# The last group's components of an inverse transform: by direct SBUF rows instead of through DRAM

## The chip, the cores and the metric

The kernel runs on one NeuronCore of a Trainium2 chip. The metric is device time in microseconds of one execution; the kernel before and the changed kernel are compared by the medians of their runs. TensorE (PE) does the matmuls, VectorE (DVE) and ScalarE (ACT) move results out of PSUM and do the elementwise work, GpSimd (POOL) helps and issues DMAs, and SyncE (SP) issues DMAs only. SP, ACT and POOL each have a DMA queue of their own.

## The reference

Two spectral layers and two MLP layers alternate on a 2048 x 1024 bfloat16 activation:

```python
def _A_ref(x, w_r, w_i):                    # spectral filter
    X = rfft2(x.astype(float32), axes=(-2, -1))
    X = X * (w_r + 1j * w_i)
    return irfft2(X, s=(S, D), axes=(-2, -1)).astype(bfloat16)

def _B_ref(x, w1, b1, w2):                  # MLP with Mish
    h = einsum("bsd,df->bsf", x, w1) + b1
    sp = log1p(exp(-abs(h))) + where(h > 0, h, 0)
    return einsum("bsf,fd->bsd", h * tanh(sp), w2)

x = A_x                                     # (1, 2048, 1024)
x = x + _A_ref(layernorm(x), A_w_r, A_w_i)
x = x + _B_ref(layernorm(x), B_w1, B_b1, B_w2)
x = x + _A_ref(layernorm(x), A_w_r, A_w_i)
x = x + _B_ref(layernorm(x), B_w1, B_b1, B_w2)
```

## The kernel before

**The spectral layer.** The two-dimensional transform is done as matmuls against tables of cosines and sines. 2048 = 16 x 128 and 1024 = 8 x 128 are split into a short and a long factor, so the forward transform and the inverse have three steps each. `s1` is the short step over both axes; its result has 128 components, 16 for each of 8 groups g. For each group, `s2` and `s3` do the long steps, the filter is multiplied in, and `i1` and `i2` undo the long steps. `i4` undoes the short step for all groups together.

**Stages of one group.** `s3` (L737) multiplies, ACT copies the result out of PSUM (L750), and four DVE operations (L754 to L761) apply the filter. `i1(g, i)` (L764; matmuls at L772) runs twice, for i = 0 and 1; each time ACT copies 1024 columns, two PSUM banks, into the buffer V (L779). `i2(g, half)` (L781; matmuls at L793 and L811) runs twice too. Half 0 makes components 0 to 7 of the group, half 1 components 8 to 15, two banks each time. ACT copies them into U (L821); for three groups, of which the last is one, DVE copies the second half (L819).

**The turn.** U has positions l on its 128 partitions and holds 16 components r of 128 values n. `i4` needs the components on the partitions: UT has partition 8r + g, and l and n along its row. So U is stored to the DRAM tensor `u_d` and read back in another order. For groups 0 to 6, `u_turn` stores all of U on SP's queue and then reads back the group before (`u_back(g - 1)`), so one group's read-back runs beside the next group's work. Group 7 has nothing to hide behind. Each of its halves is stored by ACT as soon as it is copied (`u_turn`, L830), and `u_last` (L842) reads them back by position quarters: two DMAs of two quarters each for half 0, and four DMAs of one quarter for half 1, on SP and ACT.

`i4` (L945; matmuls at L951) takes 32 positions at a time at first, with `r_ut[q]` as the resource of the q-th quarter of positions, so its first call waits for the first quarter alone.

**Order.** The order of the stages is written out by hand in `order_A`; each string is stage, group, half (5 is `i2`), and it ends "... 460 461 370 371 560 561 470 471 570 571". Every engine takes its instructions in program order[...]. `op`, `group` and `dma` compute the waits: a read waits for all writes of a resource, a write for its readers and writers, and `parts` for what was there before `begin()`.

**Around the end of the layer.** After 571, `spin(26, 0)` issues 26 matmuls of 512 columns into PSUM bank 0 whose result nobody reads (L629), so that PE doesn't idle:

```python
self.spin(26, 0)
if li == 0:
    self.op(self.pool, lambda e: e.tensor_copy(self.B1[:], self.B1h[:]), ...)
...
while self.w1_next < 28 * li + 6:
    self.load_w1(after=self.r_ut)
```

The copy of the MLP's bias B1 on POOL follows in the first layer only. The six loads of W1 on SP wait for all of UT. Then `layer_B` starts with `i4`; DVE adds its result to the residual XS (L973), takes the statistics of the layer norm, and the MLP's matmuls `mm1` (L1041) and `mm2` (L1058) follow.

**PSUM.** `pair()` deals the eight banks out as four pairs in turn; each stage's result takes a pair, and a stage waits until its pair has been read.

**A row from SBUF to SBUF** is used in one other place of the kernel: `xr_direct` (L532) moves sixteen pieces of 16 KB from 64 partitions into one partition each, over the queues of SP, ACT and POOL, at the start of the second spectral layer.

Of the kernel before, what the change touches and what calls it, by code (L numbers as in the profile page):

```python
# [7 lines left out]
P = 128  # L8
# [171 lines left out]
class KB:  # L180
# [122 lines left out]
    def build(self):  # L303
# [9 lines left out]
        with ExitStack() as es:  # L313
# [25 lines left out]
            self.r_ident, self.r_m, self.r_mt, self.r_fd, self.r_bd = (Res(n) for n in ("id", "m", "mt", "fd", "bd"))  # L339
            self.r_b1, self.r_eps, self.r_warm = Res("b1"), Res("eps"), Res("warm")  # L340
            self.r_ud = [Res(f"ud{i}") for i in range(8)]
            self.r_ud7 = [Res(f"udh{i}") for i in range(2)]
            self.r_wd = [Res(f"wd{i}") for i in range(8)]
            self.r_xnd = [Res(f"xnd{i}") for i in range(16)]
            self.npair = 0
# [322 lines left out]
    def layer_A(self, li):  # L668
# [95 lines left out]
        def i1(g, i):  # L764

            ps, banks, _ = self.pair()
            yk, bt, v = YK[(2 * g + i) % 6], BT[g % 3], V[g % 2]
            t = bt.ap[:, i, :]
            fns = []
            for c in range(4):  # L770
                for part in range(2):
                    fns.append(lambda e, c=c, part=part: e.matmul(  # L772
                        ps[:, c * 256:(c + 1) * 256], yk.ap[:, part, c * P:(c + 1) * P], t[:, (128, 0)[part]:(384, 256)[part]],
                        start=(part == 0), stop=(part == 1)))
            self.group(fns, reads=[yk.res, bt.res], writes=banks)
            if i == 0:
                v.res.begin()
            src = ps.rearrange("p (c n) -> p c n", n=P)
            self.op(act, lambda e: e.activation(v.ap[:, :, i, :], src, ACT.Copy), reads=banks, parts=[v.res])  # L779

        def i2(g, half):  # L781

            ps, banks, _ = self.pair()
# [4 lines left out]
            def cls(kd, re, im):  # L788
                t = kd * 3 * P
                for dst, stats in ((re, (0, 2)), (im, (1, 0))):  # L790
                    for part in range(2):
                        c = t + stats[part] * P
                        fns.append(lambda e, dst=dst, part=part, c=c: e.matmul(  # L793
                            dst, BD[:, c:c + P], mov(kd, part), start=(part == 0), stop=(part == 1)))
            if half == 0:
                cls(0, ps[:, 0:256], ps[:, 256:512])
                cls(1, ps[:, 512:768], ps[:, 768:1024])
            else:
                cls(2, ps[:, 0:256], ps[:, 512:768])

                t = 9 * P
                if g == 0:
                    outs = [[(i, part, (0, 2)[part]) for part in range(2)] for i in range(2)]
                else:
                    outs = [[(0, 0, 0), (0, 1, 2), (1, 0, 0), (1, 1, 2)], [(0, 0, 1), (0, 1, 0), (1, 0, 2), (1, 1, 3)]]
                for m, terms in enumerate(outs):
                    for n, (i, part, tab) in enumerate(terms):
                        for kd in range(2):
                            rows = slice(64 * kd, 64 * kd + 64)
                            dst = ps[:, 512 * kd + 256 + m * P:512 * kd + 256 + (m + 1) * P]  # L810
                            fns.append(lambda e, dst=dst, rows=rows, i=i, part=part, tab=tab, n=n, last=len(terms) - 1: e.matmul(  # L811
                                dst, BD[rows, t + tab * P:t + (tab + 1) * P], v.ap[rows, 6 + part, i, :],
                                start=(n == 0), stop=(n == last)))
            self.group(fns, reads=[v.res, self.r_bd], writes=banks)
            if half == 0:
                u.res.begin()
            dst = u.ap[:, 8 * half:8 * half + 8, :].rearrange("p a b -> p (a b)")
            if (g, half) in ((3, 1), (5, 1), (7, 1)):
                self.op(dve, lambda e: e.tensor_copy(dst, ps), reads=banks, parts=[u.res])  # L819
            else:  # L820
                self.op(act, lambda e: e.activation(dst, ps, ACT.Copy), reads=banks, parts=[u.res])  # L821
# [1 line left out]
        def u_turn(g, half):  # L823

            u = U[g % 3]
            if g == 7:
                h = slice(8 * half, 8 * half + 8)
                if half == 0:
                    u_back(6)
                self.dma(act, self.u_d[g][:, h, :], u.ap[:, h, :], f"uwh{half}", reads=[u.res], writes=[self.r_ud7[half]])  # L830
                if half:
                    u_last()
            elif half:
                self.dma(sp, self.u_d[g], u.ap, f"uw{g % 3}", reads=[u.res], writes=[self.r_ud[g]])
                if g:
                    u_back(g - 1)
# [2 lines left out]
            self.dma(sp, self.UT.ap[g:P:8, :, :], self.u_d[g].rearrange("l r n -> r l n"), f"usp{g % 3}",  # L839
                     reads=[self.r_ud[g]], parts=self.r_ut)  # L840

        def u_last():  # L842

            def back(prog, half, q, n):
                l = slice(32 * q, 32 * q + 32 * n)
                self.dma(prog, self.UT.ap[7 + 64 * half:P if half else 64:8, l, :], self.u_d[7][l, 8 * half:8 * half + 8, :].rearrange("l r n -> r l n"),
                         f"ul{half}{q}", reads=[self.r_ud7[half]], parts=self.r_ut[q:q + n])
            back(sp, 0, 0, 2)
            back(sp, 0, 2, 2)
            for q in range(4):  # L850
                back((act, sp)[q % 2], 1, q, 1)

        self.s1(li)
        Z = ring("Z", 6, 2 * K, [2, 512])
# [10 lines left out]
        for stage, g, h in self.order_A():  # L865
# [15 lines left out]
            elif stage == 4:  # L881
                i1(g, h)
                if h and g < 6:
                    load_btabs(g + 2)
            else:
                i2(g, h)
                u_turn(g, h)
        self.spin(26, 0)
        if li == 0:
            self.op(self.pool, lambda e: e.tensor_copy(self.B1[:], self.B1h[:]), reads=[self.r_b1h], writes=[self.r_b1])  # L890
        self.w1_buf = [self.alloc(f"W1_{i}", (self.W1_OFF + i * 4096, 140 * K + (i - 4) * 4096)[i > 3], [8, 256]) for i in range(6)]
# [372 lines left out]
```

## Time and profile before

| what | value |
|---|---|
| median of 3 runs | 1017.17 us (1016.41 to 1017.61) |
| the profiled execution: time, span | 1017.47 us, 1015.7 us |
| PE busy | 959.8 us, 94% of the span |
| DVE, ACT, POOL busy | 327.2, 346.8, 81.5 us |
| granted TensorE clock | full in all 40 slices |
| stretch of the change in the first layer | about 103 to 116 us |
| the same in the second layer | about 594 to 607 us |
| DMA issues of u_scratch from ACT | 4 stores of 256 KB, 4 reads of 64 KB |
| DMA issues of u_scratch from SP | 14 stores and 14 reads of 512 KB, 4 reads of 128 KB, 4 of 64 KB |

All times of the profile are microseconds from the start of the span, unless marked ns. A line such as "L772 PE MATMUL" is the source line, the engine and the operation; a DMA that an engine's queue issues is shown as SPq, ACTq or POOL with line L249, which is the helper that all DMAs go through. The chain of waits is the chain of work that ended last, each piece followed back to what released it. "ARENA" is the one SBUF tensor that holds U, V, UT and most other buffers, so U to UT directly is "ARENA<-ARENA", and U through DRAM is "u_scratch<-ARENA" and "ARENA<-u_scratch".

### The profile page before, as it was taken

What the parts mean: (1) busy time and instruction counts of PE and PEld (TensorE: products, weight loads), DVE (VectorE), ACT (ScalarE), POOL (GpSimd) and SP (SyncE); (2) the same over time, 40 slices, a digit from 0 to 9 for tenths busy, and PEclk for the clock granted to TensorE, in tenths of its full rate; (3) what the DMA queues carried; (4) which work ended last, traced back from release to release, by engine and by line L of the source; (5) the groups of instructions that cost most, each with busy time, mean ns of one, the idle gap of its engine ahead of it and who ended that gap; (6) DMA issues with size and microseconds to landing.
All of it is one profiled execution on the core that took longest, in us unless ns stands there. A gap on an engine that the chain in (4) does not pass through costs nothing.

```text
span 1015.7 us, 13823 instructions
## 1 busy us (share of the span) xinstructions
PE 959.8 (94%) x5865; PEld 506.5 (50%) x5865; DVE 327.2 (32%) x688; ACT 346.8 (34%) x482; POOL 81.5 (8%) x114
## 2 busy tenths in 40 slices
PE   0799799999999999999999988999999999999998
PEld 0576575444444444444446757644444444444443
DVE  6797469002444000033346736830011100000111
ACT  6898384340000334300019847544100024430000
POOL 3651000000000000002521100000000000000000
PEclk9999999999999999999999999999999999999999
DMA  9979823562111220002922874246411212100000
GB/s 282 245 220 319 212 66 114 178 207 73 47 46 32 73 83 21 1 21 75 206 62 78 237 189 144 85 157 207 127 25 46 74 52 79 46 1 11 21 27 26
DMA packets 154141, 106.99 MB, mean 105 GB/s; under 512 B 74384, under 2 KB 133600, under 8 KB 154080
## 3 DMA queue, kind: packets, MB, share of 16 engines
q1 hardware_dynamic: 143136, 78.88, 27.4%
q0 software_dynamic: 8912, 25.84, 8.8%
q10 hardware_dynamic: 2032, 1.39, 0.5%
q8 instruction: 47, 0.77, 0.3%
q14 instruction: 14, 0.11, 0.0%
HBM read 80.85 MB, written 20.71 MB: 100 GB/s over the span
## 4 chain that ended last, share of the span: by engine, by line
PE 86%; DVE 7%; ACT 3%; DMA 2%; issue 1%; ACTq 0%; POOL 0%; DVEq 0%
PE PS L1058 38%; PE PS L1041 37%; PE PS L772 2%; PE PS L698 2%; PE PS L793 2%; DVE BN L459 1%; DMA ARENA<-c_bt 1%; PE PS L951 1%; DVE ARENA L620 1%; ACT ARENA L549 1%; PE PS L1007 1%; DVE ARENA L593 1%; PE PS L811 1%; ACT ARENA L779 1%; PE PS L629 1%
## 5 line engine op out<-in xcount | busy, mean ns | idle before, releaser
L1041 PE MATMUL PS<-ARENA 128*128 128x512 bf16 (+1 forms) x1984 | 391.1, 358 | 0.7 <-DVE ARENA L1012 0.6
L1058 PE MATMUL PS<-ARENA 128*128 128x512 bf16 x1792 | 387.4, 379 | 0.0
L1045 ACT ACTIVATE ARENA<-PS,B 128x512 bf16<-128x512 f32 (+1 forms) x248 | 158.8, 645 | 411.0 <-PE PS L1041 410.7
L1041 PEld LDWEIGHTS PS<-ARENA 128*128 128x128 bf16 x1984 | 192.8, 98 | 193.8 <-DVE ARENA L1012 1.6
L1058 PEld LDWEIGHTS PS<-ARENA 128*128 128x128 bf16 x1792 | 175.4, 98 | 211.4
L1063 DVE TENSOR_TENSOR XS<-PS,XS 128x512 bf16<-128x512 f32 x64 | 44.3, 692 | 587.0 <-PE PS L1058 587.0
L459 DVE BATCH_NORM_STATS2 BN<-XS 128x6 f32<-128x512 bf16 x100 | 64.7, 676 | 7.5 <-DMA XS<-in_A_x_dram 6.3
L549 ACT ACTIVATE ARENA<-PS 128x1440 bf16<-128x1440 f32 (+3 forms) x26 | 28.0, 1094 | 27.0 <-DVE XS L973 23.3
L249 POOL DMA_DIRECT2D xn_scratch<-ARENA x12 | 6.5, 541 | 374.2 <-DVE ARENA L511 374.2
L772 PE MATMUL PS<-ARENA 128*128 128x256 bf16 x256 | 32.4, 273 | 4.2 <-DVE ARENA L761 3.2
L779 ACT ACTIVATE ARENA<-PS 128x1024 bf16<-128x1024 f32 x32 | 34.0, 1082 | 7.1 <-PE PS L772 7.1
L431 ACT ACTIVATE RS<-MV,EPS 128x2 f32<-128x2 f32 (+2 forms) x5 | 1.5, 298 | 97.5 <-DVE MV L462 96.2
L750 ACT ACTIVATE ARENA<-PS 128x1024 bf16<-128x1024 f32 x32 | 33.2, 1070 | 4.5 <-PE PS L746 4.5
L698 PE MATMUL PS<-FD,ARENA 128*128 128x256 bf16 (+1 forms) x256 | 31.8, 271 | 2.4 <-ACT ARENA L618 1.2
L772 PEld LDWEIGHTS PS<-ARENA 128*128 128x128 bf16 x256 | 24.2, 98 | 11.9 <-DVE ARENA L761 5.6
L754 DVE TENSOR_TENSOR ARENA<-ARENA 128x1024 bf16<-128x1024 bf16 x32 | 22.0, 688 | 21.2 <-ACT ARENA L750 21.2
L821 ACT ACTIVATE ARENA<-PS 128x1024 bf16<-128x1024 f32 x26 | 27.3, 1086 | 2.4 <-PE PS L793 2.4
L698 PEld LDWEIGHTS PS<-FD,ARENA 128*128 128x128 bf16 x256 | 24.4, 98 | 6.5 <-DVE ARENA L620 1.4
L793 PE MATMUL PS<-ARENA,BD 128*128 128x256 bf16 x192 | 24.9, 273 | 2.3 <-ACT ARENA L779 2.3
L511 DVE TENSOR_SCALAR ARENA<-XS,MV,RS 128x1024 bf16<-128x1024 bf16 x48 | 24.9, 543 | 1.0
L733 ACT ACTIVATE ARENA<-PS 128x1024 bf16<-128x1024 f32 x22 | 23.4, 1079 | 3.2 <-PE PS L698 3.2
L951 PE MATMUL PS<-MT,ARENA 128*128 128x32 bf16 (+1 forms) x512 | 20.4, 191 | 4.0 <-ACT ARENA L549 2.5
(76 smaller groups left out, 521.4 us busy)
## 6 DMA issues: line engine op xcount, KB each, us to landing
ARENA<-in_B_w_dram SPq DMA_DIRECT2D x56, 512.0 KB, 3.9
ARENA<-in_B_w_dram SPq DMA_DIRECT2D x56, 256.0 KB, 4.3
u_scratch<-ARENA SPq DMA_DIRECT2D x14, 512.0 KB, 4.7
ARENA<-u_scratch SPq DMA_DIRECT2D x14, 512.0 KB, 6.0
XS<-in_A_x_dram SPq DMA_DIRECT2D x4, 1024.0 KB, 8.7
w_scratch<-ARENA POOLq DMA_DIRECT2D x8, 512.0 KB, 5.9
ARENA<-w_scratch POOLq DMA_DIRECT2D x8, 512.0 KB, 5.1
out_dram<-XS SPq DMA_DIRECT2D x16, 256.0 KB, 2.0
```

The lines of the kernel that those rows point to most:

```text
L459: self.op(self.dve, lambda e: e.bn_stats(self.BN[:, j, 6 * h:6 * h + 6], self.XS[:, j, 512 * h:512 * h + 512]), reads=[self.r_xs[j]], part ...
L549: fn = (lambda e: e.activation(dst, src, ACT.Copy)) if scale is None else \
L698: fns.append(lambda e: e.matmul(dst, at(r), FD[:, t:t + n], start=start, stop=stop))
L750: self.op(act, lambda e: e.activation(x.ap.rearrange("p a b -> p (a b)"), ps, ACT.Copy, scale=SIG), reads=banks, writes=[x.res])
L772: fns.append(lambda e, c=c, part=part: e.matmul(ps[:, c * 256:(c + 1) * 256], yk.ap[:, part, c * P:(c + 1) * P], t[:, (128, 0)[part]:(384, ...
L779: self.op(act, lambda e: e.activation(v.ap[:, :, i, :], src, ACT.Copy), reads=banks, parts=[v.res])
L793: fns.append(lambda e, dst=dst, part=part, c=c: e.matmul(dst, BD[:, c:c + P], mov(kd, part), start=(part == 0), stop=(part == 1)))
L951: fns.append(lambda e, l=l: e.matmul(self.PS[:, bank + l // k, l % k * w:(l % k + 1) * w], self.UT.ap[:, u0 + l, :], self.MT[:, 8 * lo:8 * ...
L1041: fns.append(lambda e, db=db, bank=bank, fl=fl: e.matmul(PS[:, bank, 0:w], wb.ap[:, db, fl * P:(fl + 1) * P], x.ap[:, db, tok], start=(db ...
L1045: self.op(act, lambda e, bank=bank, ft=ft: e.activation(at.ap[:, ft, tok], PS[:, bank, 0:w], ACT.Mish, bias=self.B1[:, ft:ft + 1]), reads= ...
L1058: fns.append(lambda e, i=i, ft=ft: e.matmul(PS[:, bank, :], at.ap[:, ft, t * P:(t + 1) * P], W2[ft].ap[:, h * 512:(h + 1) * 512], start=(i ...
L1063: self.op(dve, lambda e: e.tensor_tensor(xs, PS[:, bank, :], xs, ALU.add), reads=[self.r_bank[bank]], writes=[self.r_xs[j]])
```

## The change

For group 7 the path through DRAM is taken out (`u_last` and its resource `r_ud7`), and so are its ACT stores. In its place `u_rows` sends component r of U, 128 partitions of 256 bytes, straight to partition 7 + 8r of UT, a row of 32 KB. There are sixteen such DMAs in three batches, six on SP, six on POOL and four on ACT, and each writes all four quarters of positions. The evacuations of group 7 are split by PSUM bank: bank 0 by DVE and bank 1 by ACT, in `i1` and in both halves of `i2`. In half 0 of `i2` the matmuls are cut into two groups of one bank each, and each bank's components leave when that bank is copied; half 1 stays one group. The read-back of group 6 is called ahead of `i2(7, 0)` instead of behind it, which leaves its place on SP's queue as it was. `spin` goes from 26 to 16 matmuls. Both spectral layers run this code.

```diff
--- before.py
+++ after.py
@@ -339,7 +339,6 @@
             self.r_ident, self.r_m, self.r_mt, self.r_fd, self.r_bd = (Res(n) for n in ("id", "m", "mt", "fd", "bd"))
             self.r_b1, self.r_eps, self.r_warm = Res("b1"), Res("eps"), Res("warm")
             self.r_ud = [Res(f"ud{i}") for i in range(8)]
-            self.r_ud7 = [Res(f"udh{i}") for i in range(2)]
             self.r_wd = [Res(f"wd{i}") for i in range(8)]
             self.r_xnd = [Res(f"xnd{i}") for i in range(16)]
             self.npair = 0
@@ -776,6 +775,10 @@
             if i == 0:
                 v.res.begin()
             src = ps.rearrange("p (c n) -> p c n", n=P)
+            if g == 7:
+                for b, prog in enumerate((dve, act)):
+                    self.copy(prog, v.ap[:, 4 * b:4 * b + 4, i, :], src[:, 4 * b:4 * b + 4, :], [banks[b]], [], parts=[v.res])
+                return
             self.op(act, lambda e: e.activation(v.ap[:, :, i, :], src, ACT.Copy), reads=banks, parts=[v.res])
 
         def i2(g, half):
@@ -792,9 +795,25 @@
                         c = t + stats[part] * P
                         fns.append(lambda e, dst=dst, part=part, c=c: e.matmul(
                             dst, BD[:, c:c + P], mov(kd, part), start=(part == 0), stop=(part == 1)))
+            def last_out(b, prog):
+
+                r = 8 * half + 4 * b
+                self.copy(prog, u.ap[:, r:r + 4, :].rearrange("p a b -> p (a b)"), ps[:, 512 * b:512 * b + 512], [banks[b]], [], parts=[u.res])
+
             if half == 0:
+                u.res.begin()
                 cls(0, ps[:, 0:256], ps[:, 256:512])
+                if g == 7:
+                    self.group(fns, reads=[v.res, self.r_bd], writes=banks[:1])
+                    fns = []
+                    last_out(0, dve)
+                    u_rows(u, ((sp, 0), (pool, 1), (sp, 2), (pool, 3)))
                 cls(1, ps[:, 512:768], ps[:, 768:1024])
+                if g == 7:
+                    self.group(fns, reads=[v.res, self.r_bd], writes=banks[1:])
+                    last_out(1, act)
+                    u_rows(u, ((act, 4), (sp, 5), (pool, 6), (sp, 7)))
+                    return
             else:
                 cls(2, ps[:, 0:256], ps[:, 512:768])
 
@@ -812,10 +831,13 @@
                                 dst, BD[rows, t + tab * P:t + (tab + 1) * P], v.ap[rows, 6 + part, i, :],
                                 start=(n == 0), stop=(n == last)))
             self.group(fns, reads=[v.res, self.r_bd], writes=banks)
-            if half == 0:
-                u.res.begin()
+            if g == 7:
+                last_out(0, dve)
+                last_out(1, act)
+                u_rows(u, ((pool, 8), (sp, 9), (act, 12), (pool, 10), (sp, 11), (act, 13), (pool, 14), (act, 15)))
+                return
             dst = u.ap[:, 8 * half:8 * half + 8, :].rearrange("p a b -> p (a b)")
-            if (g, half) in ((3, 1), (5, 1), (7, 1)):
+            if (g, half) in ((3, 1), (5, 1)):
                 self.op(dve, lambda e: e.tensor_copy(dst, ps), reads=banks, parts=[u.res])
             else:
                 self.op(act, lambda e: e.activation(dst, ps, ACT.Copy), reads=banks, parts=[u.res])
@@ -823,14 +845,7 @@
         def u_turn(g, half):
 
             u = U[g % 3]
-            if g == 7:
-                h = slice(8 * half, 8 * half + 8)
-                if half == 0:
-                    u_back(6)
-                self.dma(act, self.u_d[g][:, h, :], u.ap[:, h, :], f"uwh{half}", reads=[u.res], writes=[self.r_ud7[half]])
-                if half:
-                    u_last()
-            elif half:
+            if half and g < 7:
                 self.dma(sp, self.u_d[g], u.ap, f"uw{g % 3}", reads=[u.res], writes=[self.r_ud[g]])
                 if g:
                     u_back(g - 1)
@@ -839,16 +854,10 @@
             self.dma(sp, self.UT.ap[g:P:8, :, :], self.u_d[g].rearrange("l r n -> r l n"), f"usp{g % 3}",
                      reads=[self.r_ud[g]], parts=self.r_ut)
 
-        def u_last():
-
-            def back(prog, half, q, n):
-                l = slice(32 * q, 32 * q + 32 * n)
-                self.dma(prog, self.UT.ap[7 + 64 * half:P if half else 64:8, l, :], self.u_d[7][l, 8 * half:8 * half + 8, :].rearrange("l r n -> r l n"),
-                         f"ul{half}{q}", reads=[self.r_ud7[half]], parts=self.r_ut[q:q + n])
-            back(sp, 0, 0, 2)
-            back(sp, 0, 2, 2)
-            for q in range(4):
-                back((act, sp)[q % 2], 1, q, 1)
+        def u_rows(u, rows):
+
+            for prog, r in rows:
+                self.dma(prog, self.UT.ap[7 + 8 * r:8 + 8 * r, :, :], u.ap[:, r, :], f"ur{prog.name}", reads=[u.res], parts=self.r_ut)
 
         self.s1(li)
         Z = ring("Z", 6, 2 * K, [2, 512])
@@ -883,9 +892,11 @@
                 if h and g < 6:
                     load_btabs(g + 2)
             else:
+                if (g, h) == (7, 0):
+                    u_back(6)
                 i2(g, h)
                 u_turn(g, h)
-        self.spin(26, 0)
+        self.spin(16, 0)
         if li == 0:
             self.op(self.pool, lambda e: e.tensor_copy(self.B1[:], self.B1h[:]), reads=[self.r_b1h], writes=[self.r_b1])
         self.w1_buf = [self.alloc(f"W1_{i}", (self.W1_OFF + i * 4096, 140 * K + (i - 4) * 4096)[i > 3], [8, 256]) for i in range(6)]
```

`copy` is an existing helper: it issues an ACT activation for ACT and a `tensor_copy` for DVE.

## The prediction

> **What bounds the kernel now.** I read the page's chain first: 86% of the span is PE, but the change touches only the end of each spectral layer, so I followed the chain of waits in that stretch of the second layer (start us, length us, what):
>
> ```profile
> 594.45 1.06 PE PS L772 x8
> ...
> 595.54 1.03 ACT ARENA L779
> ...
> 596.70 1.47 PE PS L793 x12
> 598.17 0.57 PE PS L811 x16
> ...
> 598.77 1.24 DVE ARENA L819
> ...
> 600.03 2.26 DMA u_scratch<-ARENA
> ...
> 602.31 4.20 DMA ARENA<-u_scratch
> ...
> 606.65 0.96 PE PS L951 x32
> ```
>
> Everything is serial here: last i1 matmuls, their evacuation, i2, its evacuation, a write to DRAM, a read back, then i4 (L951). The stretch from the end of the last evacuation (600.01) to i4 is 6.64 us. The same stretch in the first layer:
>
> ```profile
> 104.49 1.03 ACT ARENA L779
> ...
> 107.64 1.24 DVE ARENA L819
> ...
> 108.93 5.80 PE PS L629 x26
> 114.73 0.30 issue
> 115.03 0.96 PE PS L951 x32
> ```
>
> There the 26 filler matmuls of `spin` end last, though the data came hardly sooner. From the first evacuation (L779) to i4 it is 10.54 us here and 11.11 us in the second layer; subtracting 491.05 us carries a time of the second layer to the first. After L951 a chain of DVE and PE work runs that no DMA ends, so what i4 gains reaches the end whole, once a layer.
>
> What a direct SBUF-to-SBUF row costs is seen at 523 us, where `xr_direct` sends 16 KB rows from three queues (timeline, then DMA issues with KB and us to landing):
>
> ```profile
> 523.70 3.76 SPq L249 DMA_DIRECT2D ARENA<-ARENA  x6
> 523.70 3.42 ACTq L249 DMA_DIRECT2D ARENA<-ARENA  x5
> 523.96 2.70 POOL L249 DMA_DIRECT2D ARENA<-ARENA  x5 [8.52 <-DVE ARENA L511]
> ```
>
> ```profile
> ARENA<-ARENA SPq DMA_DIRECT2D x6, 16.0 KB, 2.3
> ARENA<-ARENA ACTq DMA_DIRECT2D x5, 16.0 KB, 2.5
> ARENA<-ARENA POOLq DMA_DIRECT2D x5, 16.0 KB, 2.1
> ```
>
> So an issue takes 0.63 us on SP, 0.68 on ACT, 0.54 on POOL, and a row lands 2.1 to 2.5 us after its issue. While group 6 is read back (DMA view, 598 to 600 us), the engines move
>
> ```profile
> DMA packets 1661, 0.43 MB, mean 213 GB/s; under 512 B 1661, under 2 KB 1661, under 8 KB 1661
> ```
>
> [...] The old read-back has 8 partitions outermost, the new rows 128 sources; the windows view shows the DMA at 0.57 from 603.1 to 605.3, when the old reads run alone[...]. [...] The trace has full clock with 0.81 us idle ahead of i4.
>
> **The change part by part, second layer.**
>
> 1. Evacuation of i1(7,1): one ACT copy of 1024 (1.03 us) becomes a DVE and an ACT copy of 512 at once. ACT: 0.60 (L549, 128x512 from PSUM). DVE has no such row: between 0.61 (half of L819's 1.22) and 0.69 (L1063, an add of 512 from PSUM); I take 0.69. V is ready at 596.23 instead of 596.57: 0.34 saved, and i2 starts at 596.37. The pair of i1(7,0) costs nothing: the DVE copy stands behind L761, which ends at 594.40, so it ends at 595.09, while PE runs the second L772 batch to 595.51. Without that cover it would cost up to its 0.69.
>
> 2. i2 itself is the same 28 matmuls, 2.04 us, cut into groups by bank: a semaphore more, no wait. They end at 598.41 instead of 598.75. Bank 0 of the first half goes to DVE after four matmuls (597.0 to 597.7), bank 1 to ACT (597.4 to 598.0).
>
> 3. The wait that is added: on ACT's queue the issue of row 4 stands ahead of the last ACT copy. ACT is free at 598.03, the issue takes to 598.7, so the copy runs 598.7 to 599.3 instead of 598.43 to 599.03. All eight last rows wait for both copies: 599.3, against 600.01 before. Cost 0.27, or 0.5 if the issue takes 0.85.
>
> 4. DMA issues. Gone: two writes (ACT), four reads on SP and two on ACT, with 2.26 + 4.20 us on the chain. New: 16 rows of 32 KB, six on SP, six on POOL, four on ACT. SP is past its read-back of group 6 (issued at 596.19) and takes rows 0, 2, 5, 7, 9, 11 from 597.7 on, at 0.63 each: the last is issued at 600.87. POOL, idle in both stretches, issues its last at 600.8 (0.27 late at the start, as at 523.96); ACT at 600.65. Queued behind: on SP the W1 loads, which wait for all of UT as before and had 15 us to spare (issued at 608.22, mm1 at 623); on POOL in the first layer the copy of B1, some 3 us later, which the first Mish needs at about 128.
>
> 5. Landing of the last row. Unhindered, 600.87 + 2.1 to 2.3 = 603.1. [...] First packets come some 1.2 us after an issue in the trace (523.70 to 524.91)[...]. The sixteen completions of one 16 KB row at 523 are spread over 0.45 us, some 36 GB/s[...]. I take 604.2, and i4 at 604.3.
>
> 6. `spin`: 26 to 16 matmuls. One costs (5.80 - 0.38)/25 = 0.217, so 16 take 3.63. They start with DVE's bank 0, 599.16, and end at 602.8; with the 0.30 behind them, i4 cannot start before 603.1. PE then idles 1.5 us[...].
>
> Sum: i4 at 604.3 instead of 606.65, 2.35 saved; in the first layer at 113.25 instead of 115.03, 1.78. Together 4.1: 1017.47 - 4.1 = 1013.3 for the profiled execution (its span is 1015.7), which stood 0.3 above the median of the runs, 1017.17. **Forecast 1013.0.**
>
> **The rivals.**
>
> A. [...]i4 at 603.1 and 112.0, 3.5 + 3.05 saved, 1010.6. For it: the rows at 523 landed in 2.1 to 2.5 us. Against: they were half as long[...].
>
> B. The rows land about when the read-back did (i4 at 605.4 to 606.4), because issues take 0.85 to 1.17, as a few do on ACT in the trace (0.85 at 524.30)[...]. Saved 0 to 1.9: 1016.
>
> C. Slower: rows take turns. [...]i4 at 608.4 and 117.4, 1.75 + 2.35 lost, 1021.3. It decides from 0.85 us a row, where the two layers' sums meet (i4 at 606.37). For it: no row of the trace puts 32 KB into one partition. Against: at 523 rows to different partitions landed 0.6 apart on each queue without slowing.
>
> That the change doesn't do what it says is covered in A and B: all rows must land before any i4, where before a quarter was enough.
>
> **How the numbers follow.** Main case 0.52 (1012 to 1014), A 0.28, B 0.09, C 0.11. About 0.2%, 2.0 us, is what a measurement can tell from no change, so faster means under 1015.1: main and A, 0.80; same, B, 0.09; slower, C, 0.11. The range from 1010.4 takes in A with the faster DVE copy, and ends at 1016.0 within B; C and the rest of B are left out.
>
> **What would show it.** In the profile after: an ACT and a DVE copy of 128x512 side by side before i2 (step 1); ACT's last copy some 0.3 us behind DVE's (3); issues of 0.5 to 0.7 us on three queues, the last near 600.5 to 601 on the old time scale, shifted by the first layer's gain (4); ahead of i4 a wait for a DMA of ARENA to ARENA of about 1.5 us (main), or only the 0.3 us behind `spin` (A). A wait over 4 us, or landings of more than 4 us on SP, would be C. If i4 gains but the end does not, something behind i4 took it back, and the forecast is wrong in its rigid shift.

## The result, and the profile after

The changed kernel is slower. Its median is 1024.86 us over 4 runs (1023.97 to 1026.29), against 1017.39 us for the kernel before over 4 runs (1016.41 to 1019.12). The ratio is 1.0073 with an interval of [1.0053, 1.0093], so the loss is 7.4 us where a gain of 4 was forecast. The profiled execution of the changed kernel took 1026.29 us, its span 1024.5 us.

Where the time went is seen by lining up the two traces at a few points. The table has the start or end of the named work, in us from the start of each span, and how much later the changed kernel is.

| point | before | after | later by |
|---|---|---|---|
| last i1 matmul, first layer, end | 104.45 | 105.17 | 0.72 |
| first mm1 matmul, first layer, start | 125.76 | 131.30 | 5.54 |
| first i1 matmul, second layer, end | 545.44 | 551.03 | 5.59 |
| last i1 matmul, second layer, end | 595.50 | 601.09 | 5.59 |
| first mm1 matmul, second layer, start | 617.38 | 626.25 | 8.87 |
| last mm1 matmul, start | 915.33 | 924.20 | 8.87 |

The first 0.72 us was there before the change begins to act, so it is a difference between two executions. The rest is lost in the two stretches of the change alone, 4.82 and 3.28 us, and is carried to the end with no more than 0.05 us of change. So the question is only what happens between the last i1 matmul and `i4`. That distance, first layer and second, was 10.58 and 11.15 us before, was to be 8.8 in both by the forecast, and is 15.34 and 14.38. It is the measure of the experiments below that keep the structure; from i4's first matmul to mm1's first it is 10.7 to 10.8 us in each of them but one, which is named there.

The chain of waits of the changed kernel, second layer (start us, length us, what; L771 is i1, L796 and L830 are i2, L552 is the copy on DVE, L962 is i4):

```profile
600.04 1.06 PE PS L771 x8
...
601.12 0.70 DVE ARENA L552
...
601.87 1.48 PE PS L796 x12
603.36 0.57 PE PS L830 x16
...
603.95 0.70 DVE ARENA L552
604.65 0.76 SPq L249
...
607.68 0.55 SPq L249
...
608.27 7.00 DMA ARENA<-ARENA
...
615.46 1.03 PE PS L962 x32
```

Down to the last issue the chain has the steps that were worked out: V ready 0.7 us after i1's matmuls, the copies, six issues on SP, of which one took longer (step 4 below). Then one line, the landing of the last row, takes 7.00 us from its issue, more than the store and the read-back that it replaces (2.26 and 4.20 us). In the first layer's chain the same line is longer still:

```profile
110.54 9.80 DMA ARENA<-ARENA
...
120.51 1.03 PE PS L962 x32
```

The issues of that stretch of the second layer (KB each, median us from issue to landing) say that this is no single late row; all three queues are alike:

```profile
ARENA<-ARENA SPq DMA_DIRECT2D x6, 32.0 KB, 7.1
ARENA<-ARENA POOLq DMA_DIRECT2D x6, 32.0 KB, 6.9
ARENA<-ARENA ACTq DMA_DIRECT2D x4, 32.0 KB, 7.2
```

The line that says most is the DMA view of 606 to 615 us, when the rows are under way (40 slices; first the busy share of the 16 DMA engines in tenths, then what they moved):

```profile
DMA  9999999999999999999999996220000000000000
...
DMA packets 1611, 0.49 MB, mean 55 GB/s; under 512 B 1532, under 2 KB 1532, under 8 KB 1611
```

The engines are busy in every slice of the first 5.6 microseconds, yet the window's mean is 55 GB/s, and 70 GB/s from 607 to 612 us, without the idle end; with the read-back of group 6 the kernel before moved 213 GB/s, also at a full busy share. At a low rate that means that each packet takes long. The durations of the packet records say so directly (medians; SP and ACT send 256-byte packets, POOL 2048-byte ones):

| stretch | 256 B, ns | 2048 B, ns |
|---|---|---|
| before, old read-back, 603.1 to 605.3 us | 18 | none |
| after, rows, second layer, 607 to 612 us | 80 | 335 |
| after, rows, first layer, 111 to 117.5 us | 101 | 362 |

The rows hold up group 6's read-back too, which runs beside them: in the second layer it lands 9.89 us after its issue, where it was 4.94 in the kernel before.

Finally the clock. The windows view (after the stretch its length, then busy time and instructions of PE and the others, and behind POOL the granted clock, DMA share and GB/s) has PE without any work for 7 us, and about half clock afterwards:

```profile
608.40:615.40 7.00, 0.00 (x0) 0.00 (x0) 0.00 (x0) 0.00 (x0) 0.00 (x0) 0.66 0.67 35
615.40:621.00 5.60, 5.30 (x150) 5.02 (x150) 4.38 (x10) 1.79 (x3) 0.00 (x0) 0.51 0.82 237
```

The first layer has the same: 8.0 us without a matmul (112.5 to 120.5 us), then a granted clock of 0.51 from 120.5 to 126 us. In the kernel before, where PE idled 0.81 us ahead of i4 in the second layer, it was 1.00 from 606.6 to 612 us. It costs next to nothing here: from i4's first matmul to mm1's first it is 10.79 us instead of 10.73, which is i4's first call (1.03 us instead of 0.96). Behind that call the chain runs over DVE and ACT, and from 621 to 624 us the clock is full again (1.00).

### The profile page after: what moved, and what is told of

It reads as the page before. It is cut to its first block, busy times and chain, and to the rows that moved or that the text cites. A ratio compares the mean times of both kernels' runs of the same rounds, so it can differ in the third digit from the quotient of the medians.

```text
span 1024.5 us, 13727 instructions
## 1 busy us (share of the span) xinstructions
PE 951.8 (93%) x5759; PEld 506.6 (49%) x5845; DVE 331.0 (32%) x694; ACT 345.7 (34%) x484; POOL 88.0 (9%) x126
## 4 chain that ended last, share of the span: by engine, by line
PE 85%; DVE 6%; DMA 4%; ACT 3%; issue 1%; SPq 1%; POOL 0%; ACTq 0%; DVEq 0%; POOLq 0%
PE PS L1069 38%; PE PS L1052 37%; PE PS L771 2%; PE PS L697 2%; DMA ARENA<-ARENA 2%; PE PS L796 2%; DVE BN L458 1%; PE PS L962 1%; DMA ARENA<-c_bt 1%; ACT ARENA L548 1%; DVE ARENA L619 1%; PE PS L1018 1%; DVE ARENA L592 1%; PE PS L830 1%; SPq L249 1%
## 5 line engine op out<-in xcount | busy, mean ns | idle before, releaser
L548 ACT ACTIVATE ARENA<-PS 128x512 bf16<-128x512 f32 (+3 forms) x34 | 32.8, 978 | 41.8 <-DVE XS L984 30.5
L962 PE MATMUL PS<-MT,ARENA 128*128 128x32 bf16 (+1 forms) x512 | 22.0, 202 | 16.8 <-DMA ARENA<-ARENA 15.2
L771 PE MATMUL PS<-ARENA 128*128 128x256 bf16 x256 | 32.4, 273 | 4.1 <-DVE ARENA L760 3.2
L749 ACT ACTIVATE ARENA<-PS 128x1024 bf16<-128x1024 f32 x32 | 32.5, 1046 | 4.5 <-PE PS L745 4.5
L782 ACT ACTIVATE ARENA<-PS 128x1024 bf16<-128x1024 f32 x28 | 29.1, 1062 | 3.9 <-PE PS L771 3.9
L771 PEld LDWEIGHTS PS<-ARENA 128*128 128x128 bf16 x256 | 24.2, 98 | 11.8 <-DVE ARENA L760 5.5
L962 PEld LDWEIGHTS PS<-MT,ARENA 128*128 128x128 bf16 x512 | 20.0, 104 | 19.3 <-issue 16.2
L796 PE MATMUL PS<-ARENA,BD 128*128 128x256 bf16 x192 | 24.9, 273 | 1.6 <-DVE ARENA L552 1.6
L843 ACT ACTIVATE ARENA<-PS 128x1024 bf16<-128x1024 f32 x24 | 24.8, 1074 | 0.0
```

The lines of the kernel that those rows point to most:

```text
L548: fn = (lambda e: e.activation(dst, src, ACT.Copy)) if scale is None else \
L749: self.op(act, lambda e: e.activation(x.ap.rearrange("p a b -> p (a b)"), ps, ACT.Copy, scale=SIG), reads=banks, writes=[x.res])
L771: fns.append(lambda e, c=c, part=part: e.matmul(ps[:, c * 256:(c + 1) * 256], yk.ap[:, part, c * P:(c + 1) * P], t[:, (128, 0)[part]:(384, ...
L796: fns.append(lambda e, dst=dst, part=part, c=c: e.matmul(dst, BD[:, c:c + P], mov(kd, part), start=(part == 0), stop=(part == 1)))
L962: fns.append(lambda e, l=l: e.matmul(self.PS[:, bank + l // k, l % k * w:(l % k + 1) * w], self.UT.ap[:, u0 + l, :], self.MT[:, 8 * lo:8 * ...
```

## The experiments

A table first, with the measure (last i1 matmul to first i4 matmul) for every kernel that keeps the structure. Times are medians, of one run each unless a number of runs is given in the text; the row "before" is of the same four runs as above.

| kernel | first layer | second layer | time, us |
|---|---|---|---|
| before | 10.58 | 11.15 | 1017.39 |
| after | 15.34 | 14.38 | 1024.86 |
| e1_dst128: rows into 128 partitions | 9.03 | 9.82 | 1014.60 |
| e2_ports16: rows into other single partitions | 12.57 | 12.35 | 1020.64 |
| e3_noback6: no read-back of group 6 | 14.52 | 13.83 | 1023.88 |
| e4_evac_only: old path, new evacuation | 10.13 | 10.39 | 1016.58 |
| e6_onequeue: all rows on SP | 15.24 | 15.30 | 1026.33 |
| e7_pieces16k: 32 rows of 16 KB | 14.07 | 13.91 | 1023.83 |
| e8_evac_q16: DRAM path, read-backs of 16 partitions | 9.56 | 10.51 | 1015.61 |
| e9_sp_act: rows on SP and ACT | 14.25 | 14.90 | 1024.88 |
| e10_sp_pool: rows on SP and POOL | 13.13 | 14.79 | 1023.49 |

Each distance is of one profiled execution. How much it varies by itself is seen in the probes e5, e11 and e12, which leave the spectral layers of the kernel before as they are. With "before" that makes four executions of the same code: 10.58, 12.35, 12.76 and 10.32 us in the first layer, 11.15 and three times 10.40 in the second. In the first layer of e5 and e11 the mean granted clock was 0.68 and 0.69 from 104 to 109 us, where it was full in the other two, and i2's matmuls in the chain took 3.4 us instead of 2.05. No kernel of the table had half clock in that place. Without these two the distances of the same code still differ by 0.3 us in the first layer and by 0.75 in the second, so a difference of less than a microsecond between two single profiles can be chance; the argument rests on differences of 3 to 6 us. A single time says less: the 27 runs of the kernel before beside e8 lie between 1016.07 and 1022.06 us.

### Is it the destination, which partitions, or the read-back beside the rows?

**e1_dst128** sends the same sixteen DMAs with the same sources from the same queues, but into all 128 partitions of a spare buffer:

```diff
-self.dma(prog, self.UT.ap[7 + 8 * r:8 + 8 * r, :, :], u.ap[:, r, :], ...)
+self.dma(prog, self.side.ap[:, r, :], u.ap[:, r, :], ...)
```

> The changed kernel, but each of the sixteen DMAs of group 7 writes its 128 pieces of 256 bytes into 128 partitions of a spare buffer instead of one partition of UT; i4 still waits for all of them (the computation is changed: i4 takes old values for group 7). Measured: time from the start of the second evacuation of i1(7,1) to the start of i4, 15.3 and 14.3 us in the two layers of the changed kernel, 10.5 and 11.1 in the kernel before. Theory 'one partition': what costs is that sixteen engines write into one partition, so this run falls to what issue and spin allow, 7.5 to 8.5 us in both layers, some 13 us less in all than the changed kernel, about 1012. Rival 'source': reading 256 byte pieces out of SBUF, or sixteen small DMAs at all, is slow; then it stays at 14 to 15.

Measured: 9.03 and 9.82 us, 1014.6 us in one run. The prediction had 8.8, the expectation above 7.5 to 8.5. The chain, second layer:

```profile
600.86 2.75 DMA ARENA<-ARENA
...
603.81 1.00 PE PS L966 x32
```

The last row lands 2.75 us after its issue, where it was 7.00 (3.54 in the first layer, where it was 9.80), and the packets of the rows are back at 18 ns (256 B) and 97 ns (2048 B; 598.5 to 603 us). So the whole loss, and nearly all of the missing gain, hangs on the destination: each row's 128 pieces go into **one partition**. The number of DMAs, their sources and the order of the queues are the same in both. Whether it also matters which single partitions the rows go to, e1 doesn't say; e2 looks at that.

**e2_ports16** sends each row into one partition as before, but into 64(r//8) + 4(r mod 8) + 3 (3 to 31 and 67 to 95 by fours) instead of 7 + 8r (7 to 127 by eights):

```diff
-self.dma(prog, self.UT.ap[7 + 8 * r:8 + 8 * r, :, :], ...)
+p = 64 * (r // 8) + 4 * (r % 8) + 3
+self.dma(prog, self.side.ap[p:p + 1, :, :], ...)
```

> The changed kernel, but each row of 32 KB goes to one partition of a spare buffer, [...](i4 takes old values for group 7). Theory 'ports':[...] the time from evacuation to i4 falls from 15.3 and 14.3 to 8 to 9.5 us. Theory 'turns' (a row holds up the row behind it on its queue, wherever that one goes): [...]11 to 13 us.

Measured: 12.57 and 12.35 us; packets at 67 and 275 ns from 603 to 609 us. Some 2 to 3 us better than the changed kernel, and 2.5 to 3.5 worse than e1. Which partitions the rows go to seems to have a part in it, but into these, too, more than half of what separates the changed kernel from e1 is still there. The figure is above the 8 to 9.5 us of theory 'ports', by which the choice of partitions makes the whole loss. It lies in the range given for 'turns'; e6 below speaks against that theory.

**e3_noback6** leaves out the read-back of group 6 that runs ahead of the rows:

```diff
-if (g, h) == (7, 0):
-    u_back(6)
```

> The changed kernel without the read-back of group 6[...] (UT keeps old values for group 6). Theory 'read-back': the rows are slow because they start behind and among its 2048 pieces; then evacuation to i4 falls to 8 to 9 us. Theory 'turns': the rows' own time of some 9 us stays, only the start is earlier by up to 2 us: 12.5 to 14.

Measured: 14.52 and 13.83 us, 0.8 and 0.55 less than with it, which is within what single profiles differ by. So the read-back adds a microsecond at most; the rest is the rows' own.

**e4_evac_only** keeps the store to DRAM and the old read-back, and takes only the evacuations split by bank (steps 1 and 2 of the prediction; `spin` stays at 26).

> The kernel before with one part of the change: the evacuations of group 7 split by bank between VectorE and ScalarE, the path through DRAM and 26 filler matmuls kept. Both theories hold that this part is a gain, as the prediction worked it out: V 0.34 us sooner, the last evacuation 0.7 to 0.9 us sooner, so evacuation to i4 about 9.7 and 10.3 us instead of 10.5 and 11.1, 1.6 us less in all: 1015.8. If the split itself were harmful (PSUM or the added waits), 1018 or more.

Measured: 10.13 and 10.39 us, 1016.58 us over 12 runs against 1018.27 over 15 runs of the kernel before; the ratio is 0.9988 [0.9977, 0.9999]. This part is a gain of 1.2 us by the ratio, with an interval that nearly reaches zero. The trace doesn't show where: in the second layer i4 starts 0.77 us sooner than in "before", but no sooner than in the three probes (10.40). In the first, i4 starts 0.45 us sooner than in "before", but its later matmuls then wait for the later quarters, and mm1 stands where it did (21.44 us after the last i1 matmul, 21.31 before). Not all that the evacuation saves arrives, and its chain, second layer, shows where it stays:

```profile
599.11 3.21 DMA u_scratch<-ARENA
...
602.34 3.41 DMA ARENA<-u_scratch
```

The second store starts 0.9 us sooner than before (599.11, not 600.03) and lands at the same time (602.32, not 602.29). The packets of the two stores begin at 600.0 us in both kernels, when those of group 6's read-back are about to end (600.4): the stores, though issued sooner, begin to move no sooner.

### What one row costs, and several

**e5_probe** is the kernel before with rows laid singly and in small sets into a stretch of the last MLP where the DMA engines are idle. Nothing else is changed.

> The kernel before, with lone test DMAs added in the last layer's mm2, where the DMA engines are idle: 256 byte pieces from 128 partitions of XS into spare SBUF, every 12 us another case. Theory 'one partition'[...], from issue to landing: (0) one row of 32 KB into one partition 2.7 to 3.0 us, (1) the same pieces into 128 partitions 2.1 to 2.3, (2) one row of 16 KB 2.1 to 2.3, [...](7) three times 128 partitions at once 2.2 to 2.5. Rival 'slow only in a crowd' (each row is quick alone, and only the read-back of group 6 and the number in flight slow them): (0) as quick as (1)[...]. The time of the whole is that of the kernel before.

Measured, in us from issue to landing of each row (the numbers behind "into" are the partitions, one for each row):

| set | landing |
|---|---|
| one 32 KB row, one partition | 2.69 |
| the same 32 KB into 128 partitions | 1.77 |
| one row of 16 KB | 2.08 |
| three at once, SP, ACT, POOL, into 23, 31, 71 | 3.63, 2.85, 2.79 |
| three at once, SP, ACT, POOL, into 8, 9, 40 | 5.09, 4.88, 5.02 |
| three at once, 128 partitions each | 1.77, 2.15, 1.73 |
| four on ACT, into 12, 16, 24, 64 | 2.65, 2.81, 2.81, 2.80 |
| four on ACT, into 0, 1, 32, 33 | 2.64, 4.46, 4.03, 4.49 |

The first two, as the DMA issues of their windows have them:

```profile
ARENA<-XS ACTq DMA_DIRECT2D x1, 32.0 KB, 2.7
```

```profile
ARENA<-XS ACTq DMA_DIRECT2D x1, 32.0 KB, 1.8
```

Two things follow. Some sets of partitions take rows only slowly: three into 8, 9 and 40 land 4.88 to 5.09 us after their issues, three into 23, 31 and 71 after 2.79 to 3.63. Beside a lone row the two rows more cost 5.0 - 2.7 = 2.3 us, 1.15 for a row of 32 KB, about 28 GB/s. What these partitions have in common is not shown. And within one queue a row need not wait for the one ahead: four on ACT into 12, 16, 24 and 64 land 2.65 to 2.81 us after their issues. Nothing in this probe explains 7 or 9.8 us; it takes more rows.

**e11_probe16** repeats it with sets of sixteen.

> The kernel before with sets of sixteen lone 32 KB rows in the last layer's mm2, one set every 12 us, otherwise idle DMA engines. From a set's first issue to its last landing: (0) the changed kernel's order over three queues and its partitions, (1) SP and ACT, (2) SP alone, (3) SP and POOL, [...](5) three queues, each row's pieces into 128 partitions, (6) POOL alone. Theory 'POOL': 0 and 3 take 9 to 11, 1 takes 7.5 to 8.5, 2 some 12.5 by its issues. Theory 'mixing': 0, 1 and 3 all 9 to 11. Rival 'it is the traffic beside them' (read-back of group 6, its store): 0 takes 6.5 to 7.5 here[...]. Set 5: 5 to 5.5 in every theory.[...]

Measured from the first issue of a set, in us:

| sixteen rows | last issue | last landing | between first and last landing, per row |
|---|---|---|---|
| three queues, as in the changed kernel | 3.16 | 11.06 | 0.51 |
| SP and ACT | 4.68 | 11.59 | 0.56 |
| SP and POOL | 4.38 | 12.35 | 0.60 |
| POOL alone | 7.97 | 11.43 | 0.57 |
| SP alone | 9.52 | 12.33 | 0.65 |
| three queues, into the partitions of e2 | 3.49 | 11.10 | 0.52 |
| three queues, into 128 partitions | 3.13 | 4.98 | 0.21 |

This is the changed kernel's trouble without the kernel: 11.06 us for sixteen rows, 4.98 us for the same bytes from the same queues into 128 partitions. It is also the plainest view of how the two ways of being slow look. The DMA view during the first set, then SP alone, then 128 partitions:

```profile
DMA  9999999999999999999999999999999999999989
...
DMA packets 1066, 0.40 MB, mean 67 GB/s; under 512 B 971, under 2 KB 971, under 8 KB 1066
```

```profile
DMA  4024015015015015015015006006006006006006
...
DMA packets 1958, 0.45 MB, mean 52 GB/s; under 512 B 1958, under 2 KB 1958, under 8 KB 1958
```

```profile
DMA  0028469840794693069936768860079998145003
...
DMA packets 1513, 0.50 MB, mean 143 GB/s; under 512 B 1417, under 2 KB 1417, under 8 KB 1513
```

(In the first, part of the bytes is the output's store.) With three queues the engines are busy throughout, with packets of 95 ns (2048 B: 440 ns). With SP alone they are idle three quarters of the time, with packets of 18 ns, and deliver nearly as much: a row each 0.64 us, which is only SP's rate of issue. POOL alone is near its rate of issue as well (0.53 us a row). So in these sets rows into single partitions come in at one per 0.5 to 0.6 us on average, about 55 to 64 GB/s, and issuing them faster, from more queues, or into the partitions of e2 gains little. The rival that the traffic beside the rows slows them (6.5 to 7.5 us for the first set) is out.

### Queues, pieces, pile-ups

**e6_onequeue** puts all sixteen rows on SP.

> The changed kernel with all sixteen rows on SP's queue. If rows take turns within a queue[...] the time from the end of i1 to the start of i4 goes from 15.3 and 14.4 us to some 24. If the engines as a whole do one row at a time at the pace seen (some 0.6 us a row), the queue makes no difference: 14.5 to 16, near the pace of SP's own issues (16 x 0.63 = 10 us from the first).

Measured: 15.24 and 15.30 us, the changed kernel's 15.34 in the first layer and 0.9 more than its 14.38 in the second. In the first layer SP starts the issues of the sixteen rows from 106.57 to 116.83 us. The first seven stand behind the read-back of group 6 and land 0.34 us apart; the later ones land nearly as soon as a lone row, the last for instance:

```profile
116.83 2.78 DMA ARENA<-ARENA
...
119.66 1.05 PE PS L962 x32
```

One queue, bound by its issues, ends within a microsecond of three queues, bound by the landing.

**e9_sp_act** and **e10_sp_pool** leave out POOL or ACT; the rows are the same sixteen, and alternate.

> The changed kernel with POOL's six rows given to SP and ACT, eight rows each. With all rows on SP they landed as fast as it issued them, and with three queues no sooner; in the trace of the changed kernel POOL's rows travel as 96 packets of 2048 bytes, six rows of 16, the others as 256 bytes. Theory 'POOL': those large packets,[...] hold the engines up for the other queues; without them the time from the end of i1 to i4 falls from 15.3 and 14.4 us to what eight issues a queue allow, 10 to 11.5. Theory 'mixing': rows from any two queues in the same engines hold each other up; 13 to 15.[...]

> The same with ACT's rows given to POOL and SP, eight rows each. Theory 'POOL': as slow as the changed kernel or slower, 14 to 16 us from i1 to i4. Theory 'mixing': 13 to 15, the same as SP with ACT.[...]

Measured: 14.25 and 14.90 us with ACT, 13.13 and 14.79 with POOL. No pair of queues gets out of the range of 13 to 15.5 us, so it is not POOL's larger packets, nor any one queue. Long packets don't go with every wait: in e9's second layer three quarters of them keep 18 ns from 605 to 609 us, and its last row still lands 5.87 us after its issue.

**e7_pieces16k** halves each row, 64 positions at a time:

```diff
+for h in range(2):
+    l = slice(64 * h, 64 * h + 64)
-    self.dma(prog, self.UT.ap[7 + 8 * r:8 + 8 * r, :, :], u.ap[:, r, :], ...)
+    self.dma(prog, self.UT.ap[7 + 8 * r:8 + 8 * r, l, :], u.ap[l, r, :], ...)
```

> The changed kernel with every row sent as two DMAs of 64 pieces, 16 KB, the size that xr_direct uses. If it is the 128 pieces of one burst[...], the time from i1 to i4 falls to what issue allows, 32 issues on three queues, the last some 8 us after the first: 12 to 12.5 us. If the bytes into one partition are what counts, the same 14.5 to 16 us.

Measured: 14.07 and 13.91 us. Twice the issues and half the burst change it by 0.5 to 1.3 us, so the 128 pieces of one DMA are not what makes most of the loss.

**e12_pile** asked whether it is the mixing of queues that does the harm.

> The kernel before with sets of lone 32 KB rows (128 pieces of 256 bytes each, into one partition each) laid into a stretch of the last layer's second multiplication where the DMA engines are idle; [...]their data is not used. Sets: (0) a read-back-like DMA into 16 partitions and then eight rows, all on SP, so that the rows pile up behind it; (1) the same read-back on SP, then eight rows alternately on SP and ACT; (2) one row on SP and one on ACT together; (3) two and two; (4) eight rows on SP alone; (5) eight rows alternately on SP and ACT; (6) two rows on SP. Theory 'rows of different queues hold each other up, those of one queue do not': in (0) the piled-up rows land some 0.3 us apart, in (1) 0.5 to 0.6 apart on average; (2) lands later than a lone row's 2.7 us, by 0.2 to 0.5; (4) takes 7 x 0.64 + 2.7 = 7.2 us from first issue to last landing, (5) no less than about 6.3, although its last issue is some 2 us sooner. Rival 'any pile-up of rows is slow, in one queue too': (0) also 0.5 to 0.6 us a row. Rival 'it takes three queues': (1) and (5) run at 0.3 us a row, (5) is over in about 5.2 us.

Measured from the first issue of a set: (2) two rows together land at 2.63 and 3.01; (3) two and two at 4.10; (4) eight on SP at 7.29, last issue 4.51; (5) eight on SP and ACT at 6.18, last issue 2.08, with packets of 18 ns throughout. Behind a read-back, (0) eight on SP end at 8.63 with the first three landing 0.3 us apart; (1) eight on both queues end at 9.09, and the read-back itself lands at 7.09 instead of 5.13. Most of the theory's figures came out ((2), (4), the first three of (0), and nearly (5)), but they fit another reading as well, one rate for all rows together. Eight rows from two queues are sooner than from one, by 1.1 us, and hold up no engine; the last six of the eight even land within 1.3 us of each other. But of the 2.4 us that their earlier issue offered they got no more than that. Counted from the first packets, which the records have 1.1 to 1.2 us after the issue, the eight rows of (5) come in at (6.18 - 1.1)/8 = 0.63 us each, the sixteen of e11's first set at (11.06 - 1.2)/16 = 0.62; the four of (3) at 0.75, so there is a fixed part in it. With sixteen from more than one queue the backlog becomes long enough to hold the engines up: in e11's set of SP and ACT the packets of the first four rows of each queue have medians of 18 ns, those of the later ones 77 to 121 ns, but for one row at 18. One rate is the simpler account, but it is not proven: no queue issues rows much faster than they come in (SP 0.64, POOL 0.53 us a row), and where rows of one queue did pile up, in e6 and in (0), a few landed 0.25 to 0.5 us apart.

### A version that beats both

**e8_evac_q16** keeps the new evacuation and the path through DRAM, and reads back each quarter of positions with one DMA of 16 partitions, in place of two of 8. Against the kernel before, in `u_last`:

```diff
-back(sp, 0, 0, 2)
-back(sp, 0, 2, 2)
-for q in range(4):
-    back((act, sp)[q % 2], 1, q, 1)
+for q in range(4):
+    l = slice(32 * q, 32 * q + 32)
+    self.dma((sp, act)[q % 2], self.UT.ap[7:P:8, l, :],
+             self.u_d[7][l, :, :].rearrange("l r n -> r l n"), ...)
...
-self.spin(26, 0)
+self.spin(18, 0)
```

> A candidate: path through DRAM, evacuations split by bank, and the read-back of group 7 as four DMAs, one for each quarter of positions, each into all 16 partitions of the group (before: two and four DMAs into 8 partitions), with 18 filler matmuls. Theory 'one partition / few partitions': [...]the first quarter lands some 2.6 us after the second store: i1 to i4 9.2 and 9.6 us instead of 10.1 and 10.4 with the split alone, 3 us less than the kernel before: ratio 0.997. If the DMA engines have a backlog anyway, no more than the split alone: 0.999.

Measured: 9.56 and 10.51 us; 1015.61 us over 22 runs against 1017.12 over 27 of the kernel before, ratio 0.9981 [0.9973, 0.9989]. It is the fastest complete kernel of this study, 1.9 us better than before by the ratio. Its interval overlaps that of e4, so how much of this the new read-back adds to the new evacuation is not shown. Its chain, second layer:

```profile
597.71 4.05 DMA u_scratch<-ARENA
...
601.82 2.64 DMA ARENA<-u_scratch
...
604.60 0.96 PE PS L967 x32
```

The first read-back takes 2.64 us where the old one took 4.20, for a quarter of the positions each. The old reads write 8 partitions each, the new ones 16; no run varies that alone, so it is not shown to be the reason. The DMA views differ as the times do: before (600 to 607 us) the old reads keep the engines busy at some 6 tenths and move about 143 GB/s, in e8 (600 to 606 us) the new ones fill them and move 212 to 289 GB/s:

```profile
DMA  9999999983000000015435665666666666666666
```

```profile
DMA  9410000000000000000005999999999999730000
```

Against "before" i4 comes 1.0 us sooner in the first layer and 0.6 in the second, but against the three probes' 10.40 us not sooner in the second at all. The difference between the layers is in the store, 3.09 us in the first layer's chain and 4.05 in the second's. In both, the stores' last packets start 1.2 to 1.4 us behind the last ones of group 6's read-back, and in the second layer that read-back is over 1.2 us later, counted from i1.

## Why the prediction was wrong, by its steps

The measured ratio puts the time at 1024.6 us on the scale of the forecast, 11.6 above 1013.0.

**Steps 1 to 3, evacuation and i2: right.** V was ready 0.74 us after the last i1 matmul instead of 1.07, by DVE copies of 0.69 to 0.70 us, the value taken. ACT's 512 copies took 0.60, beside DVE's: after the last i1 matmul of the second layer both start at 601.12 us, each on a PSUM bank of its own. The last evacuation ended 3.7 us after i1 instead of 4.5; the prediction had 3.8. e4 puts what these steps bring alone at 1.2 us by the ratio.

**Step 4, the issues: right in the first layer, short in the second.** SP starts its last row 5.37 us after the last i1 matmul in the first layer (110.54 - 105.17); the prediction had 5.37 (600.87 - 595.50). In the second layer it is 7.18, mostly because one issue of SP, its first row, took 2.17 us instead of 0.6. e1 has the same pause in the same place (2.09 us); there the last issue is 1.47 us later than in the first layer, and i4 0.8. Its cause was not followed. In the changed kernel it can't be what set the end: the second layer, which has it, was the sooner of the two.

**Step 5, the landing: this is the step that failed.** It gave 3.3 us from the last issue to the last landing, and the chain shows 9.8 and 7.0 us in the two layers. The 3.3 was the author's estimate, in which one row, 15, waits for one other, 11. Rows that wait for each other in this way are there in e5 (1.15 us a row into 8, 9 and 40). What the step took for granted is that all the others come in side by side. They did not, not all of them: sixteen rows into the partitions 7 + 8r come in at 0.5 to 0.6 us a row (e11), and the partitions of e2 were no better there. In e11's first set the last one lands 11.1 us after the first issue; in the kernel, with group 6's read-back alongside, it is 13.0 us in the first layer and 12.0 in the second. The issues of step 4 are hidden behind that, not ahead of it. The rows at 523 us misled in the way that the prediction itself had named: they were half as long. Sixteen of 16 KB in 3.76 us of issues ask for 70 GB/s, little more than the rate found here, so hardly a backlog could build up. And the medians that were read, 2.1 to 2.5 us, hid that the last two of these rows to be issued landed 3.5 and 3.4 us after their issues.

**Step 6, `spin`: right in its length, wrong in what follows it.** The shorter spin was over at 608.3 us, 7.2 us after i1 and well before the data; the prediction had 7.3. PE idled 7 to 8 us, not 1.5, and the granted clock was 0.51 behind that; the cost was 0.06 us a layer.

**The sum and the rigid shift.** What i4 lost reached the end whole: 4.82 + 3.28 us at mm1, and 8.87 - 5.59 = 3.28 still at the last mm1 matmul.

**The rivals.** A (spin binds) and B (rows land with the old read-back) are out; i4 waits 7.1 us for the rows. C (rows take turns) has the sign, half the size, and the sign by which it was to be known (a wait of over 4 us): it put i4 at 117.4 and 608.4 on the old scale, 4.1 us lost in all, and with the measured losses of 4.76 and 3.23 it is 119.8 and 609.9. But its mechanism is not the one at work. It had the six rows of SP's queue wait for one another; e5, e11 and, behind the read-back, e6 show rows of one queue landing 0.64 us apart, nearly all of them 2.6 to 2.8 us after their issues. It is the sixteen rows together that come in at no more than one per 0.5 to 0.6 us. C was given 0.11. The argument that took it down, rows 0.6 us apart on each queue at 523 us without slowing, rested on rows of half the length.

**What stays open.** Shown is that the single destination partition makes the difference, that a long enough backlog of such rows lengthens the packets of the engines, and that no choice of queues takes the loss away. Why sixteen rows come in no faster than one per 0.5 to 0.6 us, into either set of partitions, is not settled. The records do show that part of the wait lies behind the packets: a lone row's last packet ends 1.45 us after the issue and the row lands at 2.69, while the same bytes into 128 partitions have 1.46 and 1.77. In e11's first set the last packet ends at 8.1 us and the last row lands at 11.06; into 128 partitions it is 4.66 and 4.98. The packets of all three queues lengthen together (POOL's go from 84 to 440 ns, those of SP and ACT from 18 to 95 in e11's first set), but no run here shows where they are held up. Nor is it known why e2's partitions help by 2 to 3 us in the kernel and not at all in the probe.

## What to carry to other kernels

When a transpose is done by DMA, look at how many partitions one DMA *writes*: sixteen DMAs that each spread 32 KB from 128 partitions into a single one came in at 0.5 to 0.6 us apiece, and neither more queues nor other single partitions changed that much in the probe, while a read-back of 128 KB through DRAM, with all sixteen destination partitions in one DMA, took 2.6 us. Before pricing a new transfer from a row of the profile, check that the row was loaded as heavily; the rows at 523 us, which had hardly a backlog, landed after 2.1 to 2.5 us (medians), those of the changed kernel after 6.9 to 7.2 in the second layer. In a DMA view, a full busy share at a third of the rate seen elsewhere (70 against 213 GB/s here) says that each packet takes long; here another destination shape took that away, and other queues did not.

## What was not expected of the hardware

- One partition as destination costs 0.9 us even for a lone DMA: 2.69 us for 32 KB against 1.77 into 128 partitions. The packets take equally long; the difference comes after the last of them has ended.
- When sixteen such rows stand in three queues, packets of 256 B lengthen from 18 ns to between 80 and 101 ns, and those of 2048 B from 84 ns to between 335 and 440; with eight rows in two queues they stay at 18 ns.
- A single queue whose rows come 0.64 us apart keeps the engines idle three quarters of the time and is only 1.3 us slower for sixteen rows than three queues (12.33 against 11.06 us).
- A PE idle time of 7 to 8 us went with half the clock (0.51) for the next 5 to 6 us and cost 0.06 us, since PE did not set the pace there.
